# A fused attention and feed-forward block: QKV rests as pairs of row halves in the score banks, and a third buffer for first-layer weights

## The chip, the cores and the metric

One core of one Trainium2 chip. The metric is device time in microseconds of one execution of the whole kernel, the median of several. All tensors are bf16; sums are taken in f32 in PSUM, which has eight banks.

## The reference

One sequence of S = 2048 tokens of width D = 576 goes through two layers, each behind a layer normalisation and with a residual. Cut to what matters:

```python
x = A_x                                     # 1 x 2048 x 576
h = x + A(layernorm(x)); out = h + B(layernorm(h))

def A(x):                                   # 32 heads of 18, four segments of 512 tokens
    q, k, v = x @ wq, x @ wk, x @ wv
    for s in range(4):
        p = softmax(q_s @ k_s.T * 18**-0.5 + causal mask)
        a_mem = phi(q_s) @ M / (phi(q_s) @ z + 1e-6)        # phi(t) = t + 1 if t > 0 else exp(t)
        outs.append(g * a_mem + (1 - g) * (p @ v_s))        # g = sigmoid(beta), one a head
        M += phi(k_s).T @ v_s;  z += sum(phi(k_s))
    return concat(outs) @ wo

def B(x):                                   # 4608 hidden units
    return gelu(x @ w1 + b1) @ w2 + b2
```

## The kernel before

**Tiling.** The tokens are cut into 8 chunks of 256, each of two tiles of 128 (`tl` 0 and 1; tile `t = 2c + tl`). The width 576 is four blocks of 128 rows and a rest of 64. A product with `wqkv` or `wo_t` (`mm5`, L610 to L613) is therefore five matmuls: four of 128 rows (L612) and one for the rest, 65 rows with a zero row in the weights (L613). From chunk 1 on, the 1728 columns of q, k and v are cut into four products of 432 columns.

**Streams.** Seven streams make the work, as generators:

- `stream_P(tl)` (L675): loads x, normalises it (`layernorm`, L615), transposes it to `xT` (on TensorE in chunks 0 and 1, by a transposing DMA from chunk 2 on, L367), forms the q, k, v products, each in one of the rotating PSUM banks, copies them to `qk_pad` and `v_aug` (`move`, L710 on ScalarE or L711 on VectorE), and transposes q and k by DMA to `QT` and `KT`.
- `stream_A` (L959): the attention, in 80 visits. A visit is 16 score matmuls of 32 rows (L841) into `st4`, four PSUM banks side by side, one exp over all four (L847, ScalarE) to `pt`, causal masks (L852 on GpSimd or L854 on VectorE), and later the products with v (L873 in 32 columns of the array, L886 in chunk 0) into the bank `ox`. There is one `st4`: the scores of a visit wait for the exp of the one before.
- `stream_M` (L784) sums the memory M and z; `memory_mm` (L905, matmuls L910) reads it, with `t2` as its result; `finish` (L923) scales the heads, with `t1` in between.
- `stream_B(tl)` (L1009): the product with `wo_t`, the residual, the second normalisation, its transpose `xn2T` (four buffers, one a chunk), and h to memory (`hd`).
- `stream_F1` (L1116): the first layer of B in 9 groups of 512 hidden units for each chunk. The 64-row rests of a group run as pairs on both row halves of the array (L1185, two banks a pair), the 128-row blocks after them (L1198); the bias is added in the copy out of PSUM (L1206 ScalarE, L1208 VectorE), gelu follows in larger pieces (L1220). For chunk 0 the first five groups run tile by tile (L1158, L1160 with `xz`, a zero-padded copy of the rest).
- `stream_F2` (L1228): the second layer (L1254) and the result.

In the first microseconds, where TensorE has no work yet, matmuls on the zero tile `pq` are issued into free banks (L1326).

**First-layer weights.** A group's weights are one 512 KB DMA (L1105) and two of 32 KB for the rests, one for each row half (L1108). They are loaded anew for each chunk, 72 groups in all, into two buffers `w1g`, at first with three more inside the unused `hT` of chunk 1, and at the end with three inside `wqkv`, when the last q, k, v product is done. `w1_at` says which group lies where; a load waits until the matmuls of the group that lay there before have read it.

**PSUM.** Three rotating banks, `ox`, and the four of `st4`. After the last visit `swap` (L514) turns the four into further rotating banks (`late` in the profile).

**Order.** A planner (`step`, L1282) lets the streams make numbered operations, with costs and due times (`SLACK`, `PHASES`). What is issued is then written out by hand: `arranged` (L1344) goes through the list `ORDER` and issues the operations in that order, each engine in order of the list; a negative entry takes the other engine that an operation may run on. `PLACE` gives the bank of each rotating use. All DMAs go through the SP queue in the order of the list.

```python
def arranged():
    place.update(enumerate(map(int, PLACE)))
    for i in ORDER:
        o = ops[max(i, ~i)]
        if o.ways or o.spare:
            o.eng, (o.dur, o.issue) = list((o.ways or o.spare).items())[i < 0]
        yield o
```

Of the kernel before, what the change touches and what calls it, by code (L numbers as in the profile page):

```python
# [9 lines left out]
ALU = mybir.AluOpType  # L10
# [6 lines left out]
def kernel(  # L17
# [16 lines left out]
    P = 128  # L34
# [24 lines left out]
    def sbuf(name, shape, dt=BF16):  # L59
# [1326 lines left out]
```

## Time and profile before

| what | value |
|---|---|
| time of the runs, us | 458.16, 458.70, 458.83 (median 458.70) |
| profiled execution, us | 458.34, its span 456.6 |
| TensorE busy | 448.5 us of the span, 6074 matmuls |
| ScalarE, VectorE, GpSimd busy | 315.3, 286.9, 147.4 us |
| DMA | 83.39 MB, 137491 packets; queue q1 busy for 76.5% of 16 engines |

In the lines of the profile PE is TensorE's matmuls, PEld its weight loads, DVE VectorE, ACT ScalarE, POOL GpSimd, SPq the queue that issues DMAs; L and a number is the line of the kernel. A tile is written as out<-in. In the groups, "x56 | 19.5, 348" means 56 instructions, 19.5 us of busy time together, 348 ns the mean of one; matmuls overlap, so that the mean is longer than the distance from one start to the next. In the waits, the numbers are us in total, times, and the longest. In the transfers, KB each and us from issue to landing.

### The profile page before, as it was taken

The numbers are of one execution on the slowest core, as the hardware profiler recorded it, in microseconds if no ns is written. First come the engines' busy times: TensorE is split into PE (matmuls) and PEld (weight loads), VectorE is DVE, ScalarE is ACT, GpSimd is POOL, SyncE is SP. The second block draws the span as 40 slices with busy tenths as digits, with TensorE's granted clock in tenths as the row PEclk, the third lists the DMA queues.
The fourth block names the chain that finished last, engine by engine and source line by source line (L and its number), as shares of the span: only waits on it lengthen the run. The fifth ranks groups of instructions, "written<-read, shape, count | busy, mean of one in ns | idle before, by whom it ended". The sixth has DMA issues, their size and how long they took to land.

```text
span 456.6 us, 14417 instructions
## 1 busy us (share of the span) xinstructions
PE 448.5 (98%) x6074; PEld 333.2 (73%) x6074; DVE 286.9 (63%) x761; ACT 315.3 (69%) x316; POOL 147.4 (32%) x202
## 2 busy tenths in 40 slices
PE   7999999999999999999999999999999999999997
PEld 5776776666777777776567777667788888888874
DVE  6998888887786767876765686678672532211101
ACT  5999889976887965797786876978932354366230
POOL 4776423564373033436512333233210020000000
PEclk9999999999999999999999999999999999999999
DMA  7989998969798987787796679987778767575001
GB/s 227 329 252 264 193 184 201 182 176 178 166 251 156 232 202 178 195 177 135 204 176 165 180 194 165 201 201 156 192 193 213 196 194 191 161 208 157 27 14 39
DMA packets 137491, 83.39 MB, mean 183 GB/s; under 512 B 72786, under 2 KB 135634, under 8 KB 137426
## 3 DMA queue, kind: packets, MB, share of 16 engines
q1 hardware_dynamic: 137426, 82.47, 76.5%
q8 instruction: 47, 0.77, 0.7%
q14 instruction: 18, 0.15, 0.1%
HBM read 59.43 MB, written 6.49 MB: 144 GB/s over the span
## 4 chain that ended last, share of the span: by engine, by line
PE 89%; DMA 5%; SPq 3%; ACT 1%; DVE 1%; issue 1%; ACTq 0%
PE bank L1254 21%; PE bank L1198 17%; PE bank L612 13%; PE late L1254 6%; PE late L1198 6%; PE st L841 5%; PE ox L873 4%; PE bank L613 3%; PE bank L1185 3%; PE bank L1158 2%; PE ox L1254 1%; PE ox L1198 1%; SPq L367 1%; DMA hT<-in_B_w_dram 1%; DMA w1g<-in_B_w_dram 1%; DMA beta_row<-in_A_beta_dram 1%
## 5 line engine op out<-in xcount | busy, mean ns | idle before, releaser
L847 ACT ACTIVATE pt<-st 128x2048 bf16<-128x2048 f32 x80 | 150.1, 1877 | 41.9 <-PE st L841 21.2
L1254 PEld LDWEIGHTS <-hT 128*128 128x128 bf16 x1152 | 109.4, 98 | 29.6 <-issue 0.8
L1254 PE MATMUL bank<-w_sb,hT 128*128 128x288 bf16 x864 | 126.3, 286 | 0.0
L1198 PE MATMUL bank<-xn2T,w1g 128*128 128x256 bf16 x656 | 85.3, 273 | 0.0
L852 POOL TENSOR_SCALAR_AFFINE_SELECT pt<-pt 128x512 bf16<-128x512 bf16 x81 | 52.4, 658 | 95.2 <-ACT pt L847 88.8
L1198 PEld LDWEIGHTS <-w1g 128*128 128x128 bf16 x768 | 71.4, 98 | 16.2 <-issue 6.1
L1208 DVE TENSOR_TENSOR hT<-bank,b1T 128x512 bf16<-128x512 f32 x70 | 47.3, 685 | 41.5 <-PE bank L1198 41.1
L1220 ACT ACTIVATE hT<-hT 128x1536 bf16<-128x1536 bf16 (+3 forms) x24 | 65.7, 2768 | 0.2
L612 PE MATMUL bank<-wqkv,xT 128*128 128x432 bf16 (+1 forms) x268 | 57.1, 336 | 0.9 <-DMA xT<-xn 0.8
L612 PEld LDWEIGHTS <-xT 128*128 128x128 bf16 x400 | 36.9, 97 | 19.8 <-DMA xT<-xn 0.9
L1206 ACT ACTIVATE hT<-late,b1T 128x256 bf16<-128x256 f32 x32 | 13.3, 477 | 38.7 <-PE late L1198 22.3
L1258 DVE TENSOR_TENSOR ot<-bank,hc 128x288 bf16<-128x288 f32 x24 | 11.0, 456 | 43.0 <-PE bank L1254 38.0
L1206 ACT ACTIVATE hT<-bank,b1T 128x256 bf16<-128x256 f32 x56 | 23.5, 473 | 20.1 <-PE bank L1198 20.1
L1254 PE MATMUL late<-w_sb,hT 128*128 128x288 bf16 (+1 forms) x216 | 33.9, 296 | 0.0
L841 PE MATMUL st<-QT,KT 32*128 32x128 bf16 x1280 | 32.4, 217 | 0.5 <-issue 0.5
L841 PEld LDWEIGHTS <-KT 32*128 32x128 bf16 x1280 | 18.7, 92 | 15.2 <-issue 11.9
L1198 PEld LDWEIGHTS <-wqkv 128*128 128x128 bf16 x272 | 26.0, 98 | 4.6 <-issue 0.8
L854 DVE TENSOR_TENSOR pt<-pt,causal 128x512 bf16<-128x512 bf16 x47 | 22.4, 479 | 8.3 <-ACT pt L847 8.1
L646 POOL TENSOR_TENSOR rstd_b<-rstd_b,mhalf 128x1 f32<-128x1 f32 x16 | 9.3, 582 | 56.2 <-DVE rstd_b L636 53.8
L873 PE MATMUL ox<-pt,v_aug 128*32 128x128 bf16 x1184 | 26.3, 221 | 0.0
L873 PEld LDWEIGHTS <-v_aug 128*32 128x32 bf16 x1184 | 17.2, 96 | 10.6 <-issue 8.2
L613 PE MATMUL bank<-wqkv,xT 65*128 65x432 bf16 (+1 forms) x67 | 22.6, 338 | 0.0
(156 smaller groups left out, 642.0 us busy)
## 6 DMA issues: line engine op xcount, KB each, us to landing
w1g<-in_B_w_dram SPq DMA_DIRECT2D x50, 512.0 KB, 4.1
wqkv<-in_B_w_dram SPq DMA_DIRECT2D x17, 512.0 KB, 3.9
w_sb<-in_B_w_dram SPq DMA_DIRECT2D x6, 864.0 KB, 7.7
hd<-h_t SPq DMA_DIRECT2D x14, 288.0 KB, 4.2
hc<-hd SPq DMA_DIRECT2D x28, 144.0 KB, 2.9
w1g<-in_B_w_dram SPq DMA_DIRECT2D x100, 32.0 KB, 3.2
x_b<-in_A_x_dram SPq DMA_DIRECT2D x18, 144.0 KB, 3.0
hT<-in_B_w_dram SPq DMA_DIRECT2D x5, 512.0 KB, 6.0
```

Of the source, the lines that this page charges most:

```text
L612: nc.tensor.matmul(out=out_ap, lhsT=lhsT_of(slice(0, P), k), rhs=rhs_of(slice(0, P), k), start=(k == 0), stop=False)
L613: nc.tensor.matmul(out=out_ap, lhsT=lhsT_of(slice(0, KTAIL), 4), rhs=rhs_of(slice(0, KTAIL), 4), start=False, stop=True)
L841: nc.tensor.matmul(out=st4[:, i, n * P:(n + 1) * P], lhsT=KTs[(c - c % 2 + kt // 2) % 3][rows, g, (kt % 2) * P:(kt % 2 + 1) * P], rhs=QTs[ ...
L847: op("ACT", 1.88, lambda: nc.scalar.activation(out=pt[:], in_=st4[:], func=ACT.Exp, scale=scale), sk, [("pt", slot, n) for n in range(4)], ...
L852: either(("POOL", 0.64, lambda part=part: nc.gpsimd.affine_select(out=part, in_=part, pattern=[[0, 4], [1, P]], compare_op=ALU.is_ge, fill ...
L854: ("DVE", 0.42, lambda part=part: nc.vector.tensor_tensor(out=part, in0=part, in1=causal[:].unsqueeze(1).to_broadcast([P, 4, P]), op=ALU.m ...
L873: nc.tensor.matmul(out=ox[32 * i:32 * i + 32, g % 4 * P:(g % 4 + 1) * P], lhsT=v_flat[(2 * s0 + kt) % 6][:, h * E:h * E + 32], rhs=pts[slo ...
L1198: nc.tensor.matmul(out=bank(b)[:, a * Q:(a + 1) * Q], lhsT=w1_main(wt)[:, k, (2 * (h % 2) + a) * P:(2 * (h % 2) + a + 1) * P], rhs=xn2T[c ...
L1206: nc.scalar.activation(out=hT[:, f + a, :], in_=bank(b)[:, a * Q:(a + 1) * Q], func=ACT.Identity, bias=b1T[:, f + a:f + a + 1])
L1208: either(("DVE", 0.69, lambda hT=hT, f=f, b=b: nc.vector.tensor_tensor(out=hT[:, f:f + 2, :], in0=bank(b)[:].rearrange("p (a w) -> p a w", ...
L1220: op("ACT", (f1 - f0) * Q * 0.00083 + 0.18, lambda hT=hT, f0=f0, f1=f1: nc.scalar.activation(out=hT[:, f0:f1, :], in_=hT[:, f0:f1, :], fun ...
L1254: nc.tensor.matmul(out=acc, lhsT=hT[:, q, tl * P:(tl + 1) * P], rhs=w2_sb[:, q, hs], start=(q == 0), stop=(q == NF - 1))
```

## The change

- The first-layer weights have three buffers `w1g` instead of two, and `w1_at` goes round in threes (in sixes with the three spare places). The two 32 KB DMAs of a group become one of 64 KB over all 128 partitions.
- Room for it: `xn2T` has three tiles instead of four; `ones`, `beta_row` and `b1_rows` lie in `t1`, and `xz` in `t2`, both used late.
- From chunk 3 on (`PAIRED`), the q, k, v products of a tile go to the four banks of `st4`, one product of 432 columns in each, in place of rotating banks. Their four 64-row rests come first, in two pairs, one on rows 0 to 63 and one on rows 64 to 127 of the array; then the four 128-row blocks of each product. For the second half, the rest of two weight cuts is copied to partitions 64 to 127 by two DMAs, and the normalised x has its last 64 columns a second time (`twice`).
- `BEFORE` says ahead of which visit of the attention a tile's products stand.
- After the last visit the four score banks and `ox` join the rotating ones (`dynamic_swap`).
- `ORDER` and `PLACE` are new throughout. TensorE has 6088 matmuls instead of 6074, of them 38 warm-up matmuls instead of 24; the SP queue has 348 entries instead of 418.

The diff, without `ORDER`, `PLACE` and what only renames:

```diff
-    w1_bufs = [sbuf(f"w1g{j}", [W1]) for j in range(2)]
+    w1_bufs = [sbuf(f"w1g{j}", [W1]) for j in range(3)]
-    xn2T = [sbuf(f"xn2T{j}", [KT, Q]) for j in range(4)]
+    NX = 3
+    xn2T = [sbuf(f"xn2T{j}", [KT, Q]) for j in range(NX)]
+    early = t1[:].rearrange("p h e -> p (h e)").bitcast(BF16)
+    ones, beta_row, b1_rows = early[:, 0:P], early[:, P:P + H], early[:, 2 * P:3 * P]
+    xz = t2[:].rearrange("p h e -> p (h e)").bitcast(BF16)[:, 0:2 * Q].rearrange("p (h q) -> p h q", h=2)
...
+    PAIRED = 3
+    BEFORE = {6: 22, 7: 23, 8: 27, 9: 38, 10: 45, 11: 47, 12: 52, 13: 55, 14: 62, 15: 64}
+    projected, visited = set(), [0]
...
     def stream_P(tl):
...
-                layernorm(who, xt[:], xk, xn1[tl], xnk, False, SLACK["lnp"])
+                layernorm(who, xt[:], xk, xn1[tl], xnk, False, SLACK["lnp"], twice=c >= PAIRED)
...
+            if (c, tl) == (PAIRED, 0):
+                yield need(lambda: (PAIRED - 1, 0) in half_V and (PAIRED - 1, 1) in half_V, idle=False)
+                for lo, hi in ((CH, 2 * CH), (3 * CH, 4 * CH)):
+                    dma(55, lambda lo=lo, hi=hi: nc.sync.dma_start(out=wqkv[64:P, 4, lo:hi], in_=wqkv[0:64, 4, lo:hi]),
+                        [f"wqkv{j}t" for j in range(3)], ["wqkv_pad"])
...
+            paired = c >= PAIRED
+            if paired:
+                every = [f"wqkv{j}" + e for j in range(3) for e in ("", "t")] + ["wqkv_pad"]
+                st = [("st", i) for i in range(4)]
+                yield need(lambda: visited[0] >= BEFORE[t] and all(u in projected for u in BEFORE if u < t), None, [kx] + every, st, mode=64)
+
+                def rests(xTt=xTt, cuts=cuts):
+                    for i, (lo, hi) in enumerate(cuts):
+                        rows = slice(64 * (i % 2), 64 * (i % 2) + 64)
+                        nc.tensor.matmul(out=st4[:, i, 0:hi - lo], lhsT=xTt[rows, 4, :], rhs=wqkv[rows, 4, lo:hi], start=True, stop=False,
+                                         skip_group_check=True)
+
+                op("PE", 2 * mm(CH), rests, [kx] + every, st, n=8, mode=64)
...
-                b = bank_slots.take()
-                def product(lo=lo, hi=hi, b=b, xTt=xTt):
-                    mm5(bank(b)[:, 0:hi - lo], lambda r, k: xTt[r, k, :], lambda r, k: wqkv[r, k, lo:hi])
-                op("PE", 5 * mm(hi - lo), product, [kx] + wk, [b], n=10)
+                b = ("st", ch) if paired else bank_slots.take()
+                def product(lo=lo, hi=hi, area=area, xTt=xTt, paired=paired):
+                    if not paired:
+                        mm5(area()[:, 0:hi - lo], lambda r, k: xTt[r, k, :], lambda r, k: wqkv[r, k, lo:hi])
+                        return
+                    for k in range(4):
+                        nc.tensor.matmul(out=area()[:, 0:hi - lo], lhsT=xTt[:, k, :], rhs=wqkv[:, k, lo:hi], start=False, stop=(k == 3),
+                                         skip_group_check=True)
+                op("PE", (4 if paired else 5) * mm(hi - lo), product, [kx] + wk, [b], n=10)
...
     def stream_A():
...
-                yield need(lambda: (c, qt) in half_P and (c < 2 or (c - 2, qt) in half_B) and (seg == 0 or 2 * seg - 1 in done_M),
+                yield need(lambda: (c, qt) in half_P and (c < 2 or (c - 2, qt) in half_B) and (seg == 0 or 2 * seg - 1 in done_M)
+                           and all(u in projected for u in BEFORE if BEFORE[u] <= v),
...
-    w1_at = {n: ("w1m", n % 5) if n < NG and n % 5 > 1 else ("w1", n % 5 if n < NG else (n - NG) % 2) for n in range(W1Q)}
+    w1_at = {n: ("w1m", n % 6) if n < NG and n % 6 > 2 else ("w1", n % 6 if n < NG else n % 3) for n in range(W1Q)}
...
     def load_w1(n):
...
-        for h in range(2):
-            f0 = fg * 512 + h * Q
-            dma(45, lambda h=h, f0=f0: nc.sync.dma_start(out=wt[64 * h:64 * h + 64, 4 * 512:W1], in_=B_w1[512:576, f0:f0 + Q]),
-                (), [(*k, h)], SLACK["w1"])
+        dma(90, lambda: nc.sync.dma_start(out=wt[:, 4 * 512:W1], in_=B_w1[512:576, fcols].rearrange("r (h f) -> h r f", h=2)),
+            (), [(*k, 0), (*k, 1)], SLACK["w1"])
...
-                yield need(lambda: c < 4 or c - 4 in done_F1, idle=False)
+                yield need(lambda: c < NX or c - NX in done_F1, idle=False)
```

More of the change, by code (lines that the diff above doesn't have):

```diff
@@ L453, in bank @@
         return banks["bank", place[k.serial]] if isinstance(k, Bank) else banks[k]
-    beta_row = sbuf("beta_row", [H])
-    ones = sbuf("ones", [P])
     wqkv = sbuf("wqkv", [KT, 3 * D])
@@ L517, in swap @@
         for i in range(4):
-            banks["st", i] = pool.tile([P, 512], F32, name=f"late{i}")
+            banks["bank", 3 + i] = pool.tile([P, 512], F32, name=f"late{i}")
+        banks["bank", 7] = ox
     bank_slots.free.append("ox")
@@ L613, in mm5, with layernorm @@
         nc.tensor.matmul(out=out_ap, lhsT=lhsT_of(slice(0, KTAIL), 4), rhs=rhs_of(slice(0, KTAIL), 4), start=False, stop=True)
-    def layernorm(who, src, skey, dst, dkey, f32, slack, late_scale=False):
+    def layernorm(who, src, skey, dst, dkey, f32, slack, late_scale=False, twice=False):
         fast = min(SLACK["apply"], 0) if now < 5 else SLACK["apply"]
@@ L625, in apply @@
         def apply():
-            for to, f0, f1 in ((0, 0, D), (D, 512, D))[0:2 if f32 else 1]:
+            for to, f0, f1 in ((0, 0, D), (D, 512, D))[0:2 if f32 or twice else 1]:
                 if late_scale:
@@ L650, in layernorm @@
            slack=slack + SLACK["pow"], port=False)
-        op("DVE", 0.8 if f32 else 0.43, apply, ["st" + who, skey] + ([] if late_scale else ["rs" + who]), [dkey], slack=slack + fast,
-           port=True).two = f32
+        op("DVE", 0.8 if f32 else 0.56 if twice else 0.43, apply, ["st" + who, skey] + ([] if late_scale else ["rs" + who]), [dkey], slack=slack + fast,
+           port=True).two = f32 or twice
     def transposes5(src, b):
@@ L733, in stream_P @@
                     move(va[:, v0 - 2 * H:v1 - 2 * H, 0:Dh], lambda uh=uh, n0=v0 - h0, n1=v1 - h0: uh(n0, n1), (v1 - v0) * Dh, (*vk, int(v1 == 3 * H)))
-                bank_slots.give(b)
+                if not paired:
+                    bank_slots.give(b)
                 if ch == len(cuts) - 1:
+                    projected.add(t)
                     xT_slots.give(kx)
@@ L920, in memory_mm @@
         op("DVE", 0.457, lambda: nc.vector.tensor_tensor(out=t2[:], in0=omv()[:, :, 0:Dh], in1=r2[:].unsqueeze(2).to_broadcast([P, 16, Dh]),
-                                                        op=ALU.mult), [b, "r2"], ["t2"], slack=SLACK["mem"])
+                                                        op=ALU.mult), [b, "r2"], ["t2", "xz0"] + [("xz", tl, h) for tl in range(2) for h in range(2)],
+           slack=SLACK["mem"])
     def finish(c, qt, gh):
@@ L1002, in stream_A @@
                             done_A.add(c)
-        bank_slots.free.append("ox")
-        st = [("st", i) for i in range(4)]
-        op("POOL", 0.0, swap, (), st, slack=-1000, port=False)
-        bank_slots.free += st
+        more = [("bank", 3 + i) for i in range(5)]
+        op("POOL", 0.0, dynamic_swap, (), [("st", i) for i in range(4)] + ["ox"] + more, slack=-1000, port=False)
+        bank_slots.free += more
         late.append(True)
@@ L1039, in stream_B @@
             layernorm(who, h_t[:], ("h", tl), xn2[tl], ("xn2", tl), True, SLACK["lnb"] - h0)
-            xn2T_part = xn2T[c % 4][:, :, tl * P:(tl + 1) * P]
+            xn2T_part = xn2T[c % NX][:, :, tl * P:(tl + 1) * P]
             if c < TB:
@@ L1046, in stream_B @@
                        ("DVE", 0.47, lambda b=b, xn2T_part=xn2T_part: nc.vector.tensor_copy(out=xn2T_part, in_=tview(b))),
-                   [b], [("xn2T", c % 4, tl)])
+                   [b], [("xn2T", c % NX, tl)])
                 bank_slots.give(b)
@@ L1105, in load_w1 @@
         dma(512, lambda: nc.sync.dma_start(out=w1_main(wt), in_=B_w1[0:512, fcols].rearrange("(k p) f -> p k f", p=P)), (), [k], SLACK["w1"])
[L1106 to L1109 removed]
+        dma(90, lambda: nc.sync.dma_start(out=wt[:, 4 * 512:W1], in_=B_w1[512:576, fcols].rearrange("r (h f) -> h r f", h=2)),
+            (), [(*k, 0), (*k, 1)], SLACK["w1"])
     def load_w2(j):
         dma(864, lambda: nc.sync.dma_start(out=w2_sb[:, j * 6:(j + 1) * 6, :], in_=w2v[:, j * 6:(j + 1) * 6, :]), (), [("w2", j)], SLACK["w2"])
[L1114 removed]
+    later = [lambda n=n: load_w1(n) for n in (2, 3, 4, 5)] + [lambda j=j: load_w2(j) for j in range(6)]
     def stream_F1():
@@ L1134, in stream_F1 @@
         for c in range(NCH):
-            xk = [("xn2T", c % 4, 0), ("xn2T", c % 4, 1)]
+            xk = [("xn2T", c % NX, 0), ("xn2T", c % NX, 1)]
             hT = hTs[c % 2]
@@ L1176, in stream_F1 @@
                 wk = [key for _, k in w1s for key in (k, (*k, 0), (*k, 1))]
-                yield need(lambda: c in done_B and (c < 2 or c - 2 in done_F2), bank_slots, xk + wk, mode=64, n=2 * len(some))
+                yield need(lambda: c in done_B and (c < 2 or c - 2 in done_F2) and some[-1] < w1_next[0], bank_slots, xk + wk, mode=64,
+                           n=2 * len(some))
                 bs = [bank_slots.take() for _ in range(2 * len(some))]
@@ L1185, in tails @@
                                 nc.tensor.matmul(out=bank(bs[2 * i + h])[:, a * Q:(a + 1) * Q],
-                                                 lhsT=w1s[i][0][rows, 4 * 512 + a * P:4 * 512 + (a + 1) * P], rhs=xn2T[c % 4][rows, 4, :],
+                                                 lhsT=w1s[i][0][rows, 4 * 512 + a * P:4 * 512 + (a + 1) * P], rhs=xn2T[c % NX][rows, 4, :],
                                                  start=(a == 0), stop=False, skip_group_check=True)
@@ L1198, in go @@
                                 nc.tensor.matmul(out=bank(b)[:, a * Q:(a + 1) * Q], lhsT=w1_main(wt)[:, k, (2 * (h % 2) + a) * P:(2 * (h % 2) + a + 1) * P],
-                                                 rhs=xn2T[c % 4][:, k, :], start=False, stop=(k == 3), skip_group_check=True)
+                                                 rhs=xn2T[c % NX][:, k, :], start=False, stop=(k == 3), skip_group_check=True)
                         op("PE", 4 * mm(Q), go, xk + [k], [b], n=8)
```

36 lines of the change are left out of this document (18 added, 18 removed), and 228 rows, old and new, of the table ORDER.

## The prediction

> **What bounds the kernel now.** I read the page first: busy shares, granted clock, and the engines of the chain that ended last.
>
> ```profile
> span 456.6 us, 14417 instructions
> PE 448.5 (98%) x6074; PEld 333.2 (73%) x6074; DVE 286.9 (63%) x761; ACT 315.3 (69%) x316; POOL 147.4 (32%) x202
> PEclk9999999999999999999999999999999999999999
> PE 89%; DMA 5%; SPq 3%; ACT 1%; DVE 1%; issue 1%; ACTq 0%
> ```
>
> TensorE is busy in 98% of the span, at the full clock in every slice (the 9s of PEclk), and carries 89% of the chain; no other engine is over 69%. Second, the waits of the matmul queue, which say how much of the remaining 8 us can be won:
>
> ```profile
> PE ox L1326 <- DVE maskcol L539: 2.0, 1, 2.0
> PE bank L1185 <- DMA w1g<-in_B_w_dram: 0.9, 1, 0.9
> PE bank L612 <- DMA xT<-xn: 0.8, 1, 0.8
> PE st L841 <- issue: 0.5, 1, 0.5
> PE bank L1198 <- DMA hT<-in_B_w_dram: 0.4, 1, 0.4
> PE bank L612 <- DMA xT<-o_nat: 0.3, 1, 0.3
> PE bank L550 <- DMA beta_row<-in_A_beta_dram: 0.2, 1, 0.2
> PE bank L1160 <- issue: 0.2, 1, 0.2
> ```
>
> 2.2 us of it (L1326, L550) belongs to the start, ahead of the first product. Behind that TensorE waits 0.9 + 0.8 + 0.5 + 0.4 + 0.3 + 0.2 = 3.1 us in all, of which 0.9 + 0.4 = 1.3 us is for first-layer weights. The rest, up to 456.6, is the end:
>
> ```profile
> 452.48 1.41 PE L1254 MATMUL ox<-w_sb,hT 128*128 128x144 bf16 x20
> 453.47 1.13 SPq L1265 DMA_DIRECT2D out_dram<-ot  x2
> ```
>
> The last matmul ends at 453.89; what follows is one addition and one store, 2.7 us. So the time is the start, plus all TensorE work laid end to end, plus 3.1 us of waits, plus 2.7 us. An edit is worth what it takes off TensorE's own work, plus the waits it ends, less those it makes. The profiled execution took 458.34 us, 1.74 more than its span; the runs lie at 458.16 to 458.83, median 458.70. My sum is made against 458.34. This measurement tells a change of about 0.2%, 0.9 us, from none.
>
> **The rests as pairs.** Third view: the timeline of TensorE, where start to start is what one matmul costs.
>
> ```profile
> 216.09 0.90 PE L612 MATMUL bank<-wqkv,xT 128*128 128x432 bf16 x4 [0.77 <-DMA xT<-xn]
> 216.83 0.35 PE L613 MATMUL bank<-wqkv,xT 65*128 65x432 bf16 x1
> 217.02 0.89 PE L612 MATMUL bank<-wqkv,xT 128*128 128x432 bf16 x4
> ...
> 222.26 0.40 PE L841 MATMUL st<-QT,KT 32*128 32x128 bf16 x16
> 222.59 0.39 PE L1185 MATMUL bank<-xn2T,w1g 64*128 64x256 bf16 x4
> 222.92 1.92 PE L1198 MATMUL bank<-xn2T,w1g 128*128 128x256 bf16 x16
> 224.77 0.40 PE L841 MATMUL st<-QT,KT 32*128 32x128 bf16 x16
> L613 PE MATMUL bank<-wqkv,xT 65*128 65x432 bf16 x56 | 19.5, 348 | 0.0
> L1198 PE MATMUL bank<-xn2T,w1g 128*128 128x256 bf16 x656 | 85.3, 273 | 0.0
> ```
>
> A full product of 432 columns takes (216.83 - 216.09) / 4 = 0.185 us, and its rest of 65 rows, 216.83 to 217.02, the same 0.19: a rest pays for its columns, not for its rows. Of the 56 rests 432 wide, 4 x 10 belong to the ten tiles of chunks 3 to 7. They are removed: 40 x 0.185 = 7.4 us. In their place come 20 pairs on two row halves. L1185 already runs such pairs. The sixteen products of L1198 take (1.92 - 0.273) / 15 = 0.11 each; four L1185 matmuls of the same width take 222.92 - 222.59 = 0.33 together: two pairs at 0.11 and 0.11 left over. So a pair costs one width, 20 x 0.185 = 3.7 us are added, and 3.7 us are gone.
>
> The 0.11 left over is the change of tile shape: L1185 uses two tiles of 64 rows, L1198 one of 128. The score row agrees: sixteen matmuls of half that width, four abreast, would be 4 x 0.055 = 0.22, and 222.26 to 222.59 is 0.33. The compiled instruction lists of both kernels give the order of the matmuls: TensorE changes shape 278 times before and 294 times after, although six of the ten rests stand next to other work in their shape: scores and tails that stood side by side before are parted elsewhere. 16 x 0.11 = 1.8 us. The Trainium skill, TensorEngine Tiling (Array Packing), section Key Properties, has a rule that speaks against the change: going to another tiling mode drains the array. The rows agree, with 0.11 us for each drain; by the page's section Theoretical Speedup alone, 2x for rows up to 64 and no drain in the sum, the gain would be 3.7 us and not 1.9. All other matmuls of the two lists are the same in number and width, but for warm-up (below). TensorE's work: -3.7 + 1.8 = **-1.9 us**.
>
> **The third weight buffer.** The rows of the transfers:
>
> ```profile
> w1g<-in_B_w_dram SPq DMA_DIRECT2D x50, 512.0 KB, 4.1
> w1g<-in_B_w_dram SPq DMA_DIRECT2D x100, 32.0 KB, 3.2
> ```
>
> A block takes 4.1 us from issue to landing. I added up, in both instruction lists, the TensorE work between the last matmul that reads a buffer and the first that needs its next content: 5.3 us at the least before, with many at 6 to 8; 8.8 us after. Before, a block landed in time only if the SP queue issued it within 1.2 us of the buffer coming free; after, within 4.7. The two 32 KB tails of a block become one of 64 KB, and the SP queue has 348 entries where it had 418, so what stands behind them (transposes, loads of x) is issued no later. The 1.3 us for such weights go: **-1.3 us**, bounds -1.3 and 0 (0 if something lands late just behind them). The other waits, 0.8 + 0.3 for transposed tiles and 0.5 + 0.2 of issue, I leave, with -1.8 as their bound.
>
> **The start.** "Order searched on" moves it too.
>
> ```profile
> 1.68 0.27 DVE L568 MEMSET pq<- 128x256 uint32 x1
> 2.01 0.82 PE L1326 MATMUL ox<-pq 128*128 128x256 bf16 x3 [2.01 <-DVE maskcol L539]
> ...
> 3.05 1.91 PE L1326 MATMUL bank<-pq 128*128 128x256 bf16 x8
> 4.75 0.74 PE L657 MATMUL ox<-ident,xn 128*128 128x128 bf16 x5
> 5.29 1.50 PE L1326 MATMUL bank<-pq 128*128 128x256 bf16 x10
> ...
> 7.50 0.65 PE L612 MATMUL bank<-wqkv,xT 128*128 128x288 bf16 x4
> ```
>
> A warm-up matmul of 256 columns takes (4.75 - 3.05) / 8 = 0.21 us there, twice its later 0.11: the array runs slow up to about 5.6, some 3.6 us from its first matmul. In the new lists the memset of pq is VectorE's first instruction and not its fifth, so TensorE begins near 1.25; it has 38 warm-up matmuls ahead of the first product and not 24, 19 of them ahead of the first transposes. If full speed again comes 3.6 us after the first matmul, at 4.85, then 17 of the 19 run slow, the first transposes start near 5.1, the second, eleven warm-ups later, near 6.6, and the first product, eight more later, near 7.7: +0.2 us. If it comes at 5.6 whatever the start, the product is near 8.2: +0.7. If the order fits better than I can see, -0.1. I take **+0.2**, the first. The Trainium skill, TensorE: Matmul & The Clock Gate, Part 1, says that the warm-up is about 3.4 us of activity and not a number of matmuls, in a window that runs free of the program; by its 3.4 the product would come at 7.6, which changes the sum by 0.1.
>
> **The score banks.** From chunk 3 on the products of a tile fill all four score banks, and the next scores wait until the copies have emptied them; TensorE issues in order, so all that follows waits too.
>
> ```profile
> L847 ACT ACTIVATE pt<-st 128x2048 bf16<-128x2048 f32 x80 | 150.1, 1877 | 41.9 <-PE st L841 21.2 <-PE ox L873 13.1 <-issue 1.8
> L711 DVE CAST v_aug<-bank 128x432 bf16<-128x432 f32 x7 | 4.2, 606 | 2.4 <-PE bank L613 2.4
> L710 ACT CAST v_aug<-bank 128x432 bf16<-128x432 f32 x7 | 3.7, 525 | 0.5 <-PE bank L613 0.5
> L1220 ACT ACTIVATE hT<-hT 128x4608 bf16<-128x4608 bf16 x10 | 40.1, 4039 | 0.1
> ```
>
> Ahead of the rests the exp must have read the scores: 1.88 us, plus some 0.2 to start; the new list has 2.3 to 5.2 us of other TensorE work between, so that is covered. Behind the last product comes its pass through the array (0.35, the duration of an L613 row) and one copy, 0.53 or 0.61: 1.0 us with a signal at either end, about 1.1. The list has 1.15 to 4.4 us of work from the start of the last product to the next scores; three tiles (8, 9 and 13) have 1.15 to 1.2, so the cover is bare there, and without it each costs up to one copy, 0.6. I take **+0.4 us** for the ten tiles; bounds 0 and 10 x 0.6 = 6. Not below 0, since scores never waited for the product's banks before.
>
> Costed at nothing: ten more normalisations of 64 columns on VectorE (63% busy) and two copies of 64 rows inside SBUF, issued by SP right behind chunk 2, which delay a transposed tile at most and are covered where it has 2 us or more of other TensorE work ahead of it; three xn2T tiles instead of four, since chunk c needs F1 of chunk c - 3, and the list has 23 us or more of work between; the shared t1 and t2, whose early readers end 10 us ahead of the first new writer.
>
> **Sum:** 458.34 - 1.9 - 1.3 + 0.2 + 0.4 = 455.74, so **455.7**.
>
> **The rivals.** *Every wait goes*: the shorter SP queue also ends the waits for transposed tiles and the start comes no later: 458.34 - 1.9 - 3.1 = 453.3. For it: all 3.1 us are single short waits. Against: half of them are no weights. *Only TensorE's work shrinks*: the weight waits come back as others and the start loses 0.7: 458.34 - 1.9 + 0.7 + 0.4 = 457.5, no measurable change. *The score banks bind*, the one on the slower side. In ScalarE's new order three copies out of the score banks (tiles 9, 11, 14) stand right behind gelu pieces of 4.04 us. If a piece runs half its length late, TensorE stands before the next scores for that: 3 x 2.0 = 6.1, and 458.34 - 1.9 - 1.3 + 0.2 + 6.1 = 461.4. It decides once new waits exceed 0.4 + 2.6 + 0.9 = 3.9 us, 1.3 for each of the three. For it: by the lists the products hold the banks for some 65 us in all. Against: ScalarE is 69% busy, and in the lists these three tiles have their products spread over 7 to 9 us. [...] *The pairs run one after the other*, so that the change doesn't do what it says: +3.7, 459.4. The L1185 row speaks against it.
>
> **How the numbers follow.** Forecast 0.57, every wait goes 0.15, only the work shrinks 0.10, score banks 0.14, no pairing 0.04. Faster: 0.57 + 0.15 = 0.72; same 0.10; slower 0.14 + 0.04 = 0.18. The range leaves out the last two, 0.18. Low end: 453.3 less the 0.3 by which runs differ, 453.0. High end: 457.5 with two bare tiles' copies more, 2 x 0.6, 458.7.
>
> **What would show it.** Right: the pair line starts its two halves within some 10 ns, four matmuls in about 0.45 us; L613's successor has 16 rows 432 wide; no wait of TensorE for w1g; scores waiting for copies 0.4 us or less. Wrong: a wait of the score line for the copies or the exp of over 1 us in a tile, a first product behind 8 us, or new waits for transposed tiles.

## The result, and the profile after

The changed kernel takes 476.4 us (median of 6 runs, 473.7 to 478.7) where the kernel before took 458.1 beside it (6 runs): a ratio of 1.0396, 95% interval 1.0354 to 1.0439. The forecast was 455.7 in a range of 453.0 to 458.7. The change makes the kernel 4% slower. All times below are medians without the five executions of the record that ran in a slower state, one of them at a clock of 0.755.

The page of the changed kernel (profiled execution 477.96 us), with the lines that answer to those of before:

```profile
span 476.2 us, 14338 instructions
PE 454.8 (95%) x6088; PEld 334.3 (70%) x6088; DVE 286.2 (60%) x787; ACT 314.4 (66%) x302; POOL 147.2 (31%) x199
PEclk9999999899999999999999999989999999999999
PE 62%; DMA 7%; DVE 4%; issue 2%; ACT 2%; SPq 1%; POOL 0%; DVEq 0%; ACTq 0%
```

TensorE fell from 98% to 95% of a longer span, from 89% to 62% of the chain, and two slices have an 8 in the clock. No other engine has become the bound: DVE, ACT and POOL are all at a lower share than before. So TensorE waits: it is idle for 476.2 - 454.8 = 21.4 us of the span, where it was for 8.1. Its busy time grew too, by 6.3 us, although the change takes work off it; the clock has a part in that (see the last section). Its waits:

```profile
PE st L747 <- DVE qk_pad L718: 3.9, 6, 1.0
PE bank L611 <- DMA xT<-o_nat: 3.2, 1, 3.2
PE bank L1287 <- DVE hT L1241: 2.2, 1, 2.2
PE st L873 <- ACT qk_pad L717: 1.4, 2, 0.8
PE bank L1359 <- DVE pq L567: 1.2, 1, 1.2
PE st L747 <- ACT qk_pad L717: 1.2, 2, 0.9
PE st L873 <- DMA KT<-qk_pad: 1.1, 1, 1.1
PE st L747 <- ACT v_aug L717: 1.0, 2, 0.6
PE bank L1218 <- DMA w1g<-in_B_w_dram: 0.6, 1, 0.6
PE bank L1192 <- DMA w1g<-in_B_w_dram: 0.4, 1, 0.4
```

Two kinds stand out. L747 (the full products in the score banks) waits for copies out of them: 3.9 + 1.2 + 1.0 = 6.1 us in ten places. And things that a DMA feeds come late: the transposed attention output (3.2), K (1.1), and the bias add hT (2.2), which VectorE did late, since it had itself stood 3.9 us for the transposing DMA of o_col.

The first kind in the timeline of one projection:

```profile
95.13 0.54 PE L729 MATMUL st<-wqkv,xT 64*128 64x432 bf16 x4
95.60 1.63 PE L747 MATMUL st<-wqkv,xT 128*128 128x432 bf16 x8
97.27 0.52 ACT L717 CAST v_aug<-st 128x432 bf16<-128x432 f32 x1 [2.05 <-PE st L747]
97.84 0.89 PE L747 MATMUL st<-wqkv,xT 128*128 128x432 bf16 x4 [0.61 <-ACT v_aug L717]
98.82 0.46 DVE L718 CAST qk_pad<-st 128x288 bf16<-128x288 f32 x1 [1.59 <-ACT ek L928]
99.33 0.89 PE L747 MATMUL st<-wqkv,xT 128*128 128x432 bf16 x4 [0.60 <-DVE qk_pad L718]
```

The pairs do what they should: four rests in 95.60 - 95.13 = 0.47 us. Two products follow (x8). The v copy reads bank 3, which the first of the two has filled, but starts only when the second, into bank 2, is done. The third product, into bank 1, which nobody reads, starts when that copy of bank 3 ends; the fourth when the copy of bank 2 ends. In the compiled program the waits say the same: `st4` is one tile of four banks, and every access by another engine is ordered behind the last one to the tile, whatever the bank. Products and copies of one projection take turns.

### The profile page after: what moved, and what is told of

Read it like the earlier page. It is cut to its first block, busy times and chain, and to the rows that moved or that the text cites. A ratio compares the mean times of both kernels' runs of the same rounds, so it can differ in the third digit from the quotient of the medians.

```text
span 476.2 us, 14338 instructions
## 1 busy us (share of the span) xinstructions
PE 454.8 (95%) x6088; PEld 334.3 (70%) x6088; DVE 286.2 (60%) x787; ACT 314.4 (66%) x302; POOL 147.2 (31%) x199
## 4 chain that ended last, share of the span: by engine, by line
PE 62%; DMA 7%; DVE 4%; issue 2%; ACT 2%; SPq 1%; POOL 0%; DVEq 0%; ACTq 0%
PE bank L1287 16%; PE bank L1231 14%; PE late L1287 7%; PE late L1231 5%; PE st L747 5%; DMA o_col<-oT 3%; PE st L873 3%; PE ox L905 3%; PE bank L1218 2%; PE bank L611 2%; DMA KT<-qk_pad 1%; PE ox L1287 1%; PE ox L1231 1%; DVE qk_pad L718 1%; DMA x_p<-in_A_x_dram 1%
## 5 line engine op out<-in xcount | busy, mean ns | idle before, releaser
L1231 PE MATMUL bank<-xn2T,w1g 128*128 128x256 bf16 x688 | 90.3, 273 | 0.0
L1231 PEld LDWEIGHTS <-w1g 128*128 128x128 bf16 x816 | 75.5, 98 | 17.6 <-issue 6.1
L884 POOL TENSOR_SCALAR_AFFINE_SELECT pt<-pt 128x512 bf16<-128x512 bf16 x75 | 49.5, 671 | 106.0 <-ACT pt L879 90.9
L747 PE MATMUL st<-wqkv,xT 128*128 128x432 bf16 x160 | 34.3, 347 | 6.0 <-DVE qk_pad L718 3.9
L1287 PE MATMUL late<-w_sb,hT 128*128 128x288 bf16 (+1 forms) x252 | 39.1, 295 | 0.0
L611 PEld LDWEIGHTS <-xT 128*128 128x128 bf16 x240 | 22.0, 98 | 13.4 <-DMA xT<-o_nat 4.0
L747 PEld LDWEIGHTS <-xT 128*128 128x128 bf16 x160 | 14.9, 97 | 19.8 <-issue 10.3
L1239 ACT ACTIVATE hT<-late,b1T 128x256 bf16<-128x256 f32 x24 | 10.1, 473 | 28.3 <-PE late L1231 28.3
L1231 PEld LDWEIGHTS <-wqkv 128*128 128x128 bf16 x240 | 23.0, 98 | 4.0 <-issue 0.8
L1091 POOL TENSOR_TENSOR h_t<-h_t,b_bc 128x576 f32<-128x576 f32 x16 | 21.0, 1314 | 14.6 <-DVE xn L629 13.5
L973 POOL TENSOR_TENSOR o_nat<-t,t 128x288 bf16<-128x288 f32 x14 | 11.1, 794 | 43.6 <-DVE t L971 41.2
L1241 DVE TENSOR_TENSOR hT<-late,b1T 128x512 bf16<-128x512 f32 x15 | 10.3, 684 | 23.5 <-PE late L1231 23.5
```

The source lines that it names most:

```text
L611: nc.tensor.matmul(out=out_ap, lhsT=lhsT_of(slice(0, P), k), rhs=rhs_of(slice(0, P), k), start=(k == 0), stop=False)
L747: nc.tensor.matmul(out=area()[:, 0:hi - lo], lhsT=xTt[:, k, :], rhs=wqkv[:, k, lo:hi], start=False, stop=(k == 3), skip_group_check=True)
L884: either(("POOL", 0.64, lambda part=part: nc.gpsimd.affine_select(out=part, in_=part, pattern=[[0, 4], [1, P]], compare_op=ALU.is_ge, fill ...
L1231: nc.tensor.matmul(out=bank(b)[:, a * Q:(a + 1) * Q], lhsT=w1_main(wt)[:, k, (2 * (h % 2) + a) * P:(2 * (h % 2) + a + 1) * P], rhs=xn2T[c ...
L1239: nc.scalar.activation(out=hT[:, f + a, :], in_=bank(b)[:, a * Q:(a + 1) * Q], func=ACT.Identity, bias=b1T[:, f + a:f + a + 1])
L1241: either(("DVE", 0.69, lambda hT=hT, f=f, b=b: nc.vector.tensor_tensor(out=hT[:, f:f + 2, :], in0=bank(b)[:].rearrange("p (a w) -> p a w", ...
```

## The experiments

All times stand beside the kernel before on the same chip (medians 459.0 to 459.8; it was 458.1 beside the changed kernel). The runs were made on several chips, so where two kernels of different runs are compared, the difference of their medians and that of their ratios to the kernel before can differ by 1 or 2 us. Line numbers shift by some lines between variants: L624 and L761 are the products (L611 and L747 above), L888 the scores, L365 the transposing DMAs; the names of the tiles tell the rest (bank<-xn2T,w1g is F1, bank<-w_sb,hT F2, hT the bias add of F1).

**1. Four tiles instead of one.** own_four gives the four banks to the projection as four tiles and to the scores as one. The rests call `st_open(True)`, the scores `st_open(False)`:

```diff
+    def st_open(pairs):
...
+            st.pool.__exit__(None, None, None)
+        st.n += 1
+        st.pool = tc.tile_pool(name=f"st{st.n}", bufs=1, space=PSUM)
+        p = st.pool.__enter__()
+        st.ones = [p.tile([P, 512], F32, name=f"sto{i}") for i in range(4)] if pairs else None
+        st.four = None if pairs else p.tile([P, 4, 512], F32, name="st4")
```

> The changed kernel in the same order of operations, but the four score banks are one four-bank tile only while scores are in them; for the QKV products of chunks 3 to 7 they are four tiles of one bank each, as the product banks are in the kernel before. Nothing else differs, no instruction is added. Theory A (the products and the copies of one projection run in lockstep, since every access of another engine to the one four-bank tile is ordered behind the last, whatever the bank; TensorE idles for it about 30 us against 8 us before, some 12 us of that directly at L747 and at the scores behind the copies, the rest as transposes, a gelu and a clock drop that follow from lateness): the waits at L747 for copies go, and the time falls to 454 to 460 us. Rival B (the new order, the DMA traffic of the second copy of the weights' rests and the third w1 buffer set the loss; the lockstep only fills time that would be lost anyway): 468 to 477 us.

Measured: 472.5 us (6 runs, 467.6 to 474.2), ratio 1.026 (1.0217 to 1.0303). The waits at L747's place for copies are gone from the trace, but only 4 us with them (6 by the ratios, 1.0396 to 1.026): other waits have grown, most of them behind a DMA:

```profile
PE bank L624 <- DMA xT<-o_nat: 4.6, 3, 2.8
PE bank L1233 <- DMA w1g<-in_B_w_dram: 2.2, 2, 1.6
```

Theory A, the lockstep as the cause of nearly all, falls; rival B's range holds the time. Three more kernels ran beside it.

own_two, `p.tile([P, 2, 512], ...)` twice in place of the four:

> As own_four, but two tiles of two banks each: products and copies are ordered with each other inside a pair of banks only. Theory A: about a third to a half of the lockstep stays, 459 to 470 us, between own_four and the changed kernel. Rival B: as own_four within 2 us, and both above 468 us.

Measured: 473.4 us (470.0 to 474.5). That is within 1 us of own_four, as B said.

own_nopair, own_four without the rests (`for i, (lo, hi) in enumerate(())`) and with five products a chunk:

> own_four without the pairs: the eight 64-row rests of a projection are not issued, each chunk is the sum of five full products (K = 128, 128, 128, 128, 65) as before. Theory A with the prediction's term for the pairs (20 x 0.185 us saved, 16 more tile-shape switches at 0.11 us): 1.9 us over own_four, bounds 0 to 3.7 us. Rival C (the rests on both row halves do not overlap, or the switches cost more than they save): equal to own_four or faster than it.

Measured: 476.5 us, 4 over own_four and just above the bounds of 0 to 3.7: the pairs are a gain, if anything a larger one than forecast (experiment 5).

copies_last, the one tile kept, and each projection's copies moved behind its last product in the order:

> The changed kernel with its one four-bank tile; only the order written out by hand differs: the copies of a paired projection (and the transposing DMA behind them, where one lay among them) stand behind the last of its four products. So no product can wait for a copy, but the copies still follow one another, one bank at a time, and the scores behind them wait for all. Theory A: the waits at L747 for copies are gone, the waits at the scores grow by up to 1 us for each of the 10 projections; 458 to 470 us, faster than the changed kernel. Rival B: no faster than the changed kernel (474 to 480 us), since the copies only come later.

Measured: 484.8 us, worse than either theory gave. Its products no longer wait for copies, but the scores wait 3.0 + 1.0 + 0.7 + 0.6 us for copies, and the transposed output 4.4 (3.2 in the changed kernel): the copies only come later.

**2. Without the later weight loads.** Is it the DMAs? Three kernels load each first-layer group once; the 63 later loads are left out, so the products read old weights:

```diff
-        dma(512, lambda: nc.sync.dma_start(out=w1_main(wt), ...
+        dma(512, lambda: n < NG and nc.sync.dma_start(out=w1_main(wt), ...
```

(and the same for the rests).

> own_four, but the first-layer weights are loaded once only: the 63 later loads of a group (512 KB and its 64 KB of rests) are not issued, and the products read what lies in the buffers. Same instructions on every other engine. Theory D (in own_four the shared banks are off the list, and the 13 us that it is still slower than the kernel before are transposing DMAs and weight loads that land late, since they stand in one queue behind bunched w1 loads): without that traffic it reaches 449 to 457 us, and is no slower than before_now1. Rival E (the new order of the work itself, on TensorE, ACT and DVE, leaves the idle time): still 8 us or more above before_now1.

> The kernel before with the same left out (w1 groups loaded once, no later load issued): the control. It waits for DMAs some 2 us only, so 453 to 459 us by either theory.

> The changed kernel, four-bank tile and all, with the same left out. What the one tile for four banks costs by itself, without DMAs that come late: theory A says 4 to 14 us over four_now1 (the waits at L747 and at the scores stay, some 12 us in the changed kernel's trace); rival: within 2 us of four_now1, since own_four brought 4 us only.

Measured: 457.5, 456.2 and 467.5 us. Two things follow. With four tiles and without these loads the changed kernel is within 1.3 us of the kernel before treated alike: nearly all of the 13 us that own_four lost hang on the loads. That is theory D, though 457.5 lies 0.5 us above its range and isn't "no slower"; rival E, 8 us or more, falls. In the kernel before the same loads cost 459.7 - 456.2 = 3.5 us, so they are dear only in the changed one. And the lockstep by itself costs 467.5 - 457.5 = 10.0 us, not 4; with the loads it hides behind lateness that is there anyway. The longest waits of after_now1, copies ahead of products and of scores, with one for hT between:

```profile
PE st L747 <- DVE qk_pad L718: 4.4, 8, 1.0
PE bank L1190 <- DVE hT L1196: 1.7, 1, 1.7
PE st L873 <- ACT qk_pad L717: 1.4, 2, 0.8
```

**3. The joined rest DMA.** The change loads the 64 rest rows of a group, both halves, by one DMA of 64 KB in place of two of 32 KB. four_split takes that back in own_four, after_split in the changed kernel; before_join makes that one edit in the kernel before:

```diff
-            dma(45, lambda h=h, f0=f0: nc.sync.dma_start(out=wt[64 * h:64 * h + 64, 4 * 512:W1], in_=B_w1[512:576, f0:f0 + Q]),
+            dma(45, lambda h=h: h or nc.sync.dma_start(out=wt[:, 4 * 512:W1], in_=B_w1[512:576, fcols].rearrange("r (h f) -> h r f", h=2)),
```

> own_four with the 64 KB of rests of a w1 group loaded by two DMAs of 32 KB again, as in the kernel before, at the same place of the queue; all else as in own_four. If the single DMA with its rearranged rows lands late or clogs the queue, 3 us or more are won; if the 63 more issues of about 0.55 us on SP cost as much as they relieve, 470 to 475 us, no change.

> The kernel before with one change only: the two 32 KB rests of a w1 group in one DMA of 64 KB with rearranged rows, as the changed kernel loads them. If that DMA by itself slows the issues behind it (34 of 92 transposing DMAs took over 1.5 us to issue in own_four, 11 in four_split, 19 in the kernel before): 460 to 463 us, 1 to 4 us slower than before, and more than 25 such issues. Rival (the DMAs that one load less gives back to SP make up for it): within 1 us of before.

> before_join once more, for a profile at full clock (the first one ran at 0.755 throughout). The time is expected at 471 to 480 us again. If the 64 KB rest DMAs themselves take more of the DMA engines (their packets' time was 369.5 us per engine in own_four and 338.9 in four_split, 349.3 in the kernel before): 360 us or more of packet time, and TensorE's new waits are for w1g and for transposing DMAs, 8 us or more together. If not: below 353 us of packet time, and the loss has another place.

> The changed kernel, one four-bank tile and all, with the rests of a w1 group as two DMAs of 32 KB again: the fourth corner of the square (four banks or one tile, one or two rest DMAs). If the two causes add up: 2 to 3 us under the changed kernel, 472 to 475 us. If the lockstep hides what the rest DMAs cost: as the changed kernel, 475 to 479 us.

Measured: before_join 473.4 (two executions) and, run again as before_join2, 474.2 us (472.1 to 475.0), ratio 1.0323 (1.0294 to 1.0352): **this edit alone makes the kernel before 15 us slower**, several times what I expected. four_split 470.0 (ratio 1.0195, 1.0149 to 1.024), on the edge of its two expectations; after_split 476.1 (1.0369, 1.035 to 1.0388).

What the joined DMA does, first in the page's part on the DMA queues (packets, MB, share of 16 engines' span), of the kernel before and of before_join2:

```profile
q1 hardware_dynamic: 137426, 82.47, 76.5%
```

```profile
q1 hardware_dynamic: 135266, 82.46, 82.0%
```

and of own_four and four_split:

```profile
q1 hardware_dynamic: 135426, 82.57, 78.7%
```

```profile
q1 hardware_dynamic: 137586, 82.58, 72.3%
```

The same bytes take 0.765 x 456.6 = 349 us of an engine on average before and 0.820 x 473.3 = 388 joined; 0.787 x 469.5 = 370 in own_four and 0.723 x 468.8 = 339 split. Why, the steps of the DMAs' semaphores show, which the trace records. A 32 KB rest DMA has 16 steps. A joined one has three, all 72 of the changed kernel: the one issued at 56.78 us has a step at 57.82, at once, and two 5 us later, at 62.80 and 62.82. The Trainium skill, DMA: Bandwidth & Descriptors, section "Why a DMA increments its semaphore by 16 and not by 1", has the rule: each engine that takes part makes a step when its data has landed, the number of engines is the largest up to 16 that divides the slowest dimension of both sides, and the others' steps are written at once. The rearranged source has 2 there, so a joined DMA runs on two engines by this rule; the three steps of the trace agree. No run has a joined DMA on 16 engines, so that the two engines do the harm, and not the joining as such, is read from the steps and not tested. Taking the last step before a semaphore's next DMA as the landing, mean us from issue:

| kernel | rest DMA | main, 512 KB | 92 transposing DMAs |
|---|---|---|---|
| before | 3.5 | 4.7 | 3.8 |
| before_join2 | 5.4 | 5.5 | 4.7 |
| changed | 5.0 | 5.3 | 4.3 |
| own_four | 5.1 | 5.4 | 4.4 |
| four_split | 3.2 | 4.9 | 3.9 |
| four_now1 / before_now1 | | | 3.1 / 3.2 |

With joined rests the main loads and the transposing DMAs land later on average, and the issue of a transposing DMA takes longer: 34 of 92 hold SP for over 1.5 us in own_four and 33 in before_join2, where it is 11 in four_split and 19 in the kernel before. Two of the six rows of the transposing DMAs on SP (ns min/median/max), own_four and then four_split:

```profile
L365 SPq DMA_TRANSPOSE xT<-o_nat x14: 1200/1548/2335, 61.7 to 378.0; - x14
L365 SPq DMA_TRANSPOSE xn2T<-xn x14: 1199/1431/3718, 88.7 to 401.6; - x14
```

```profile
L365 SPq DMA_TRANSPOSE xT<-o_nat x14: 1199/1228/1663, 60.8 to 378.0; - x14
L365 SPq DMA_TRANSPOSE xn2T<-xn x14: 1199/1224/1294, 87.8 to 401.3; - x14
```

In before_join2 the lateness meets TensorE in w1 waits of 3.3 + 3.1 us and a transposed tile of 1.8:

```profile
PE bank L1184 <- DMA w1g<-in_B_w_dram: 3.3, 3, 1.5
PE bank L1197 <- DMA w1g<-in_B_w_dram: 3.1, 2, 1.9
PE bank L612 <- DMA xT<-o_nat: 1.8, 1, 1.8
```

Together that is 8.2 us, where the kernel before had 0.9 + 0.4 + 0.3. Waits of 0.7 to 1.5 us for hT, which VectorE did late, add 4.4, and 3.4 us ran at a granted clock of 0.50.

In the changed kernel the joined DMA costs far less than that: splitting wins 2.5 us with four tiles (3.0 by the ratios) and 0.3 with one (1.2), where products wait for copies in any case. So it is shown as a cause in the kernel before; undoing it alone brings the changed kernel little.

**4. The order of the queue.** four_split has rests and transposing DMAs as prompt as before, no lockstep, less TensorE work, and is still 10 us slower than the kernel before. Its largest waits, and VectorE's:

```profile
PE bank L1307 <- DVE hT L1261: 5.2, 1, 5.2
PE bank L624 <- DMA xT<-o_nat: 2.1, 2, 1.8
PE bank L1251 <- DMA w1g<-in_B_w_dram: 1.8, 1, 1.8
```

```profile
DVE r L980 <- DMA o_col<-oT: 7.0, 1, 7.0
```

and SP's timeline there:

```profile
297.99 3.02 SPq L1158 DMA_DIRECT2D wqkv<-in_B_w_dram  x2
301.10 1.23 SPq L365 DMA_TRANSPOSE xn2T<-xn  x1
302.38 1.23 SPq L1158 DMA_DIRECT2D wqkv<-in_B_w_dram  x2
303.70 2.29 SPq L1158 DMA_DIRECT2D w1g<-in_B_w_dram  x2
306.04 0.58 SPq L543 DMA_DIRECT2D x_b<-in_A_x_dram  x1
306.72 0.37 SPq L1107 DMA_DIRECT2D hd<-h_t  x1
307.18 1.22 SPq L365 DMA_TRANSPOSE o_col<-oT  x1
```

The source of o_col was done by 298.9 us, as VectorE's timeline has it:

```profile
298.17 0.69 DVE L977 CAST oT<-ox 128x512 bf16<-128x512 f32 x1 [0.25 <-PE ox L920]
```

From 298.0 on six rest DMAs stand before it in the one queue, besides a transposing DMA, a load of x and a store of h. VectorE waits 7.0 us for it with bias adds behind, and F2 waits 5.2 for those. Six kernels move first-layer loads in SP's queue, by an edit in the walk over `ORDER` (cut to what it does, `n` and `e` told in the comment):

```diff
+        for o in [of_(i) for i in ORDER if of_(i).reload is not None]:
+            # position n of the load; e: that of the next (previous) transposing DMA, none of its readers (writers) between
+            order.insert(e, order.pop(n))
```

Back, behind the next one or two transposing DMAs:

> own_four with the w1 loads of all but the first nine groups moved back in the order: each behind the next transposing DMA of SP's queue (101 of the 126 loads move; a load is never moved past its reader). Theory D, sharpened (the loads stand ahead of transposing DMAs in the one in-order queue, so those land late; the third buffer gives the loads the room to go later): 462 to 469 us, 3 us or more under own_four. Rival F (the queue is full either way, and what is not late as a transposing DMA is late as a weight load): 470 to 476 us.

> The same, each load behind the next two transposing DMAs. Theory D: as four_late1 or better, 458 to 468 us, unless the products then wait for the weights themselves; Rival F: slower than own_four, 474 us or more.

> four_late1 with the rests of a w1 group as two DMAs of 32 KB, as in four_split. If order in the queue and the size of the rest DMAs are two causes that add up: 2 us under four_late1, 459 to 467 us. If they are the same cause: as the better of four_late1 and four_split.

Measured: 532.7, 565.1 and 512.3 us. Theory D as I had sharpened it is wrong, and badly; rival F named the kind of wait, but the first two lie far above its 470 to 476 us as well. four_split_late1's waits are for the weights:

```profile
PE bank L1241 <- DMA w1g<-in_B_w_dram: 11.6, 10, 4.1
PE late L1254 <- DMA w1g<-in_B_w_dram: 9.9, 1, 9.9
PE bank L1254 <- DMA w1g<-in_B_w_dram: 7.8, 5, 2.6
```

A load behind a transposing DMA also waits for that DMA's source: in four_split_late1 SP stood up to 15.0 us at one for its xn, and up to 12.3 for rstd_b. Split against joined is worth 20 us here (512.3 to 532.7), and the weights are now what is waited for.

Forward:

> four_split with the w1 loads of all but the first nine groups moved forward in the order, each ahead of the transposing DMA that stood before it in SP's queue, where the last reader of the buffer still stands before that place (70 loads move). Moving them back cost 42 us (four_split_late1 against four_split), nearly all of it waits for w1g. If the new order issues the loads too late for the third buffer's room, forward wins what back lost in part: 461 to 467 us. If loads and transposing DMAs are each other's price in one queue: 468 to 476 us, with the waits for xT, KT and hT grown.

> The same, each load ahead of up to two transposing DMAs (117 steps). Too late loads: as early1 or 1 to 3 us better. Each other's price: slower than early1, 472 us or more, since a load that waits for its buffer now holds up more of the queue.

Measured: 492.5 and 494.4 us, 22 and 24 over four_split, far above the 468 to 476 us expected if each is the other's price; the step from one to two can't be told from the noise. Now it is the transposed tiles, and what VectorE makes from them:

```profile
PE st L890 <- DMA KT<-qk_pad: 3.3, 2, 1.8
PE bank L626 <- DMA xT<-o_nat: 3.1, 2, 2.6
PE bank L1310 <- DVE hT L1264: 2.8, 1, 2.8
PE bank L1241 <- DMA xn2T<-xn: 2.7, 1, 2.7
```

Last, only the rests of groups 45 to 50, those of the stall above:

> four_split with the rests of w1 groups 45 to 50 alone moved back in the order, behind the next two transposing DMAs. In four_split TensorE stood 5.2 us at 305.9 us for the bias add of F1, and that for the transposing DMA o_col, issued at 307.2 us though its source was done at 298.9 us: three of these rests stood before it in the queue. If the new order's place of these loads is what costs there: 461 to 466 us. If something else is then late in the same place: 468 us or more.

Measured: 468.9 us (467.9 to 469.5). The wait for hT fell from 5.2 to 2.7 us, and w1 waits of 2.0 + 1.2 + 0.4 stand where there were 1.8: "something else is then late".

So loads and transposing DMAs are each other's price in SP's queue, and moved all together the loads can go neither way by one transposing DMA. That the last 10 us of four_split hang on the loads is shown by experiment 2 (470.0 with them, 457.5 without; 3.5 us in the kernel before). Why the changed kernel pays so much more for them stays open: no run tells the new order, the third buffer and the DMAs that were added apart, and a kernel in the new order with two buffers was not run.

**5. The pairs alone.** four_now1 without the pairs:

> four_now1 (four one-bank tiles, w1 groups loaded once, the 63 later loads left out) without the pairs: each chunk of a QKV projection from chunk 3 on is five full products again. With the queue out of the way this prices the pairs by themselves. The prediction's term: 20 x 0.185 us saved less 16 more tile-shape switches at 0.11 us = 1.9 us, so 459.4 us against four_now1's 457.5, bounds 457.5 to 461.2. By own_nopair against own_four (476.5 to 472.5): 461.5 us.

Measured: 460.9 us (10 runs) against 457.5 (9 runs): the pairs are worth **3.4 us** (4.0 by the ratios, give or take 1.4).

No kernel that loads all its weights beats the kernel before.

## Why the prediction was wrong, step by step

Two of the signs that it named as wrong came, a first product behind 8 us and new waits for transposed tiles; the pair line came as the right sign had it, two halves 3 ns apart and four rests in 0.47 us.

**The third weight buffer** (-1.3) holds the first step that failed: "the two 32 KB tails of a block become one of 64 KB ... so what stands behind them is issued no later". I counted entries of the queue, and the number of engines that each runs on was in neither bound. The DMA takes 5.0 us to land instead of 3.5 and delays what is behind; alone, in the kernel before, it costs 15 us, and in the changed kernel some 0.3 to 3. The w1 waits that were to vanish, 1.3, are 0.6 + 0.4 = 1.0. The slack of 8.8 us of work before a load is needed was worked out for the loads and not for what shares their queue: SP still stood 44 us in all at first-layer loads whose buffer TensorE had not yet read (54 before), and everything behind them stood with it. Weights were late for 1.0 us, transposed tiles for 3.2 + 1.1 + 0.2.

**The score banks** (+0.4, bounds 0 and 6) failed as a mechanism: I looked for the wait where the next scores start, and took the four banks as four things that come free one by one. They are one tile. The wait stands at the products, 6.1 us, and the whole is 10.0 us where nothing else is late, above my upper bound. The rival that the score banks bind (461.4) had the right resource and the wrong reason: not a copy behind a gelu, but each copy between two products.

**Costed at nothing:** what the new order does to the queue, by size the largest error. 12.5 us of four_split hang on its weight loads, which cost 3.5 in the kernel before. That a late transposed tile is "covered where it has 2 us or more of other TensorE work ahead of it" looks at TensorE's list and not at the queue that feeds it: in four_split one o_col was issued 8 us after its source was done.

**TensorE's work** (-1.9) was right in kind and in its unit. A block of four rests takes 0.375 us and a switch where it has one, (40 - 20) x 0.187 = 3.7 us are saved. The trace of four_now1 has 296 changes of tile shape, that of nopair_now1 290, and that of the kernel before 280: the pairs add 6 of the 16, the others belong to the order. 3.7 - 6 x 0.1 = 3.1, measured 3.4.

**The start** (+0.2, other value +0.7): the other value, by luck.

```profile
8.17 0.65 PE L611 MATMUL bank<-wqkv,xT 128*128 128x288 bf16 x4
```

The first product starts at 8.17 us, 0.67 later than before. But up to the second transposes, at 6.59 us, the start went as for +0.2 (6.6), and it lost the rest in the last warm-up matmuls. Nor can 0.67 be called a price of the change: in the profiles the same start has its first product at 7.73 us in after_split and 9.08 in own_four, and the start of the kernel before has it at 7.50, but at 8.17 in before_now1 and before_join2. The eleven warm-up matmuls between the transposes took 1.20 us here and 1.71 in own_four, so the array ran slow longer there; neither "3.6 us after the first matmul" nor "at 5.6" holds from run to run.

How it sums, with the later loads left out: 456.2, less 3.4 for the pairs, plus a remainder of 4.7, is four_now1's 457.5 (the start gives nothing here, 8.26 us against 8.17). About 1.0 of the remainder is the ten other changes of tile shape; the rest I haven't taken apart. The lockstep then makes 467.5 of it, and the loads, 8.9 us more, make 476.4. With four tiles the loads would be 15.0: the two hide each other in part. Without the lockstep (own_four) or with the rests split (after_split) the change is still slower than before.

## What to carry to other kernels

Before two DMAs are joined, look at the slowest dimension of both sides: a rearranged source that begins with 2 ran on two engines here, and the DMAs queued behind it landed later. When buffers that were separate tiles become one, ask what the generated waits order, bank by bank in the compiled program; a plan that keeps books per bank doesn't bind them. And here, with TensorE at 98% and the DMA engines at 76.5%, the order of the DMA queue was a second bound that the lists of TensorE's work didn't show: take the loads out once, and see what is left.

## What was not expected of the hardware

The issue of a DMA itself can take long: a transposing DMA holds SP for 1.2 us at the least and for 3.7 at the most in own_four, and one for 4.6 in four_split, where no rests are joined. And a short wait costs more than its length. After the 2.18 us for hT, TensorE ran at half rate for a while: in the changed kernel's timeline products of F2 take (2.96 - 0.29) / 11 = 0.24 us each, where (1.14 - 0.29) / 7 = 0.12 each was the rule a little earlier. The granted clock was 0.50 from 319.0 to 322.3 us, and again from 86.9 to 90.2, behind the wait of 3.2 us; the profile of the kernel before has no such stretch in its work. A wait of 1.6 us in after_split was followed by one, waits of 1.6 us in own_four and 1.8 in four_split were not.

```profile
312.02 1.14 PE L1287 MATMUL bank<-w_sb,hT 128*128 128x288 bf16 x8
318.72 0.90 PE L1287 MATMUL bank<-w_sb,hT 128*128 128x288 bf16 x4 [2.18 <-DVE hT L1241]
319.68 2.96 PE L1287 MATMUL bank<-w_sb,hT 128*128 128x288 bf16 x12
```
